# A gated linear attention with an expert layer on one core: the fourth head pair packed into unused partitions, and a new written order

## The chip, the cores and the metric

The kernel runs on one core of a Trainium2 chip. Its time is the device time in microseconds, median over runs. The engines are PE (TensorE, with PEld for its weight loads), DVE (VectorE), ACT (ScalarE), POOL (GpSimd) and SP (SyncE, which here issues every transfer).

## What is computed

```python
state = zeros((4, 8, 48, 48))                        # batch, heads, 48 x 48
for t in range(768):
    state = alpha[:, :, t, :, None] * state + einsum('bhd,bhe->bhde', k[:, :, t], v[:, :, t])
    y[:, :, t] = einsum('bhd,bhde->bhe', q[:, :, t], state)
x = y.transpose(0, 2, 1, 3).reshape(3072, 384)       # float32
h = x @ w_in                                         # w_in 384 x 2048, float64
g = h * erf(maximum(h, 0) + log1p(exp(-abs(h))))
out = (g @ w_out).astype(float32)                    # w_out 2048 x 384, float64
```

## The kernel before

**Attention.** The recurrence is cut into 24 chunks: 2 pairs of batches by 12 stretches of 64 tokens. A chunk holds 2 batches and the 8 heads as 4 head pairs. Rows of k, q and alpha lie on partitions, two halves of 64, of which 48 carry a head's rows and 16 are unused; the 512 columns are 4 pairs x 2 batches x 64 tokens. `la`, `lq`, `lv` load tiles `A`, `kq`, `raw_v`. `a1` is a scan along the tokens (DVE, L239). `a2` has three ACT steps (Relu with a sum, Ln, Exp with a sum: L245, L203) and three DVE products, of which the last, L257, makes the keys in `kq`; `a3` makes the queries (L262). `a4` multiplies keys by queries pair by pair into `pS` (PE, L277), and the chunk before's keys by its values into `pu` (L286); then DVE brings the state `T` up to date (L302, L304) and masks `pS` into `sT` (L307), PE transposes the keys (`pn`, L315) and ACT copies them out (`kn`, L320). `a5` forms the chunk's outputs `py` (PE, L343) from `T`, the queries, `sT` and `raw_v`, splits them in two parts `x_hi` (ACT, L369) and `x_lo` (DVE, L373), and two chunks make a block of 256 tokens.

**Expert layer.** Each of 12 blocks has 4 groups `g` of 512 hidden columns in two halves. A step `H` is 18 PE products `ph` (L407: three for each of 3 row tiles of w_in and 2 column tiles) and a copy `hs` (ACT, L415); `U`, `L1`, `L2`, `G`, `Z` are tanh, two logarithms and an exponential, and products on ACT and DVE; `O` splits the result in `gh` (L460 on DVE or L462 on ACT) and `gl` (DVE, L465) and makes 12 PE products `acc` (L476): per tile of 128 tokens `gh` by `wo_hi`, `gh` by `wo_lo`, `gl` by `wo_hi`. Eight steps `O` make the output of a block, and `out` copies and stores it. Where the text says the **seventh O**, it means the seventh step `O` in PE's queue, counted from the start of the program.

**Weights.** w_in comes in 12 pieces of 128x512, w_out in 16 of 128x384, as 64-bit words. `weight()` loads a piece (`wst`), ACT turns the high words into float32 (L502), DVE shifts the low words (L505) and joins them in two steps (L509, L513), ACT rounds to the high part (`wi_hi`, `wo_hi`, L518), DVE subtracts for the low part (`wi_lo`, `wo_lo`, L520).

**Order.** A table `SCHED` names the steps one after another; each name runs its step up to the next `yield`. This sets every engine's queue. `lq`, `wst`, `wbuf`, `hs`, `s`, `w`, `t` share 19 buffers of one pool, `A` has 3 buffers, `raw_v` 2, and PSUM holds 2 tiles for `ph` and 4 for attention.

Of the kernel before, what the change touches and what calls it, by code (L numbers as in the profile page):

```python
# [25 lines left out]

SCHED = """
la_0 a1_0 a2_0 la_1 a2_0 a2_0 la_2 a1_1 a1_2 lq_0 a3_0 a2_0 wi_9 wi_9 wi_9 a2_0 wi_9 wi_5 wi_5 wi_5 a2_1 a2_1 a2_0
a4_0 wi_11 wi_11 wi_9 wi_11 wi_9 wi_5 wi_11 wi_8 wi_8 a2_1 wi_8 wi_0 wi_0 lv_0 wi_0 wi_5 a4_0 a5_0 a4_0 wi_0 a2_1 wi_4
wi_4 wi_4 wi_9 a5_0 a5_0 a5_0 wi_10 wi_10 wi_10 a2_1 wi_8 a4_0 lq_1 a3_1 a2_1 wi_5 wi_11 wi_1 a2_2 a2_2 wi_1 wi_1 wi_4  # L30
wo_0 a2_2 a2_2 wi_11 wi_11 lq_2 a2_2 wi_4 wi_4 wi_2 wi_2 wi_2 wo_2 wo_5 wo_5 wi_1 a4_1 wo_13 a4_1 a4_1 a4_1 wi_0 wi_0
lv_1 a5_1 wi_4 wi_2 wi_1 wi_1 a5_1 a5_1 wo_5 wi_8 wi_3 a4_1 wi_3 wo_5 wi_6 wi_2 wi_3 wi_2 wi_1 a5_1 a5_1 lq_3 wi_0
wi_2 a5_0 H_0_0_0 wi_6 wi_3 wi_6 a2_2 a3_2 a4_2 wo_1 wo_1 wo_1 wi_5 wo_4 H_0_0_1 H_0_0_1 wi_8 la_3 wo_11 wo_11 wo_11
wi_3 wi_3 a1_3 a2_3 a2_3 a2_3 a4_2 a4_2 wi_10 wo_5 wo_5 wo_13 wo_2 wi_10 H_0_0_0 H_0_0_0 wi_3 wi_10 a2_3 wo_11 a2_3
a4_2 a4_2 wo_1 wi_7 wi_7 wi_7 H_0_0_1 wi_10 wo_7 wo_7 wo_7 wo_4 wo_4 lv_2 a5_2 wi_8 wo_4 wo_0 wo_0 wo_13 a3_3 a5_2
a5_2 a5_2 H_0_1_1 U_0_0 lv_3 wi_6 H_0_1_0 H_0_1_0 H_0_1_0 a2_3 H_0_1_1 H_0_1_1 U_0_1 L1_0_1 la_4 a1_4 a2_4 a2_4 wo_10
H_0_3_1 H_0_3_1 wo_2 H_0_3_1 wo_10 wo_10 H_0_3_0 a4_3 a5_2 wo_2 wi_6 wo_2 wi_7 wo_4 wi_7 wi_7 H_0_3_0 H_0_3_0 wo_0
a4_3 a4_3 a2_4 lq_4 a3_4 a4_3 a4_3 wi_7 wi_6 a2_4 wi_6 a5_3 a2_4 wo_13 wo_0 a2_4 L1_0_0 a5_3 H_0_2_0 a5_3 L1_0_1 a5_3
L1_0_1 L1_0_0 wo_0 L1_0_0 la_5 a1_5 a2_5 a2_5 a2_5 wo_7 H_0_2_0 H_0_2_0 wo_0 a5_3 L2_0_1 wo_5 wo_4 lv_4 a4_4 a4_4 a4_4
a4_4 a4_4 a2_5 L2_0_1 H_1_2_1 H_1_2_1 wo_4 wo_3 G_0_1 lv_5 Z_0_1 L2_0_0 H_0_2_1 H_0_2_1 wo_1 H_0_2_1 U_0_2 a5_4 a5_4  # L40
a5_4 wo_3 wo_3 H_1_2_1 L2_0_0 lq_5 wo_3 H_1_0_1 H_1_0_1 G_0_0 Z_0_0 a5_4 a2_5 H_1_1_1 wo_2 H_1_0_1 H_1_1_1 Z_0_0 a3_5
O_0_0_0 H_1_1_1 a2_5 wo_11 U_0_3 L1_0_2 H_1_0_0 H_1_0_0 H_1_0_0 wo_1 L1_0_2 H_1_1_0 L1_0_3 wo_10 wo_11 O_0_0_0 Z_0_1
la_6 wo_2 H_1_1_0 O_0_0_1 H_1_1_0 a4_5 H_1_3_1 H_1_3_1 a1_6 H_1_3_0 H_1_3_0 a2_6 wo_7 L1_0_2 O_0_0_0 wo_7 wo_3 a2_6
a2_6 wo_13 wo_13 wo_11 wo_6 a4_5 a4_5 wo_10 a4_5 wo_6 a4_5 H_1_3_1 a5_5 a5_5 wo_1 O_0_0_0 O_0_0_1 O_0_0_1 wo_3 L2_0_2
wo_3 O_0_0_1 a2_6 a5_5 a5_5 a5_5 wo_9 a5_4 H_2_1_0 H_2_1_0 L1_0_3 wo_8 wo_10 wo_10 L1_0_3 wo_6 H_1_3_0 L2_0_3 H_1_2_0
G_0_3 wo_6 H_2_1_0 wo_7 H_1_2_0 la_7 H_2_3_1 H_2_3_1 wo_6 wo_13 L2_0_2 O_0_1_0 wo_6 wo_6 O_0_1_1 a2_6 O_0_1_0 O_0_1_1
lq_6 lv_6 a1_7 O_0_1_0 O_0_1_0 O_0_1_1 O_0_1_1 G_0_2 U_1_0 L2_0_3 L1_1_0 wo_9 wo_9 a2_6 H_1_2_0 H_2_2_0 H_2_2_0 wo_14
wo_14 wo_14 a3_6 a4_6 H_2_3_1 L1_1_0 wo_8 wo_8 wo_9 L1_1_0 Z_0_2 wo_8 Z_0_2 H_2_1_1 H_2_1_1 a2_7 a2_7 a2_7 wo_14 U_1_3
H_2_1_1 a4_6 a4_6 wo_8 wo_8 Z_0_3 O_0_2_0 O_0_2_1 a4_6 a4_6 a5_6 lq_7 a3_7 wo_8 H_2_2_0 wo_12 wo_9 la_8 wo_9 O_0_2_0
a5_6 a5_6 U_1_2 a2_7 L2_1_0 G_1_0 wo_9 H_2_0_1 H_2_0_1 H_2_0_1 O_0_2_1 H_2_2_1 H_2_2_1 H_2_2_1 wo_12 O_0_2_0 L2_1_0  # L50
a5_6 wo_12 O_0_2_0 wo_12 U_1_1 a2_7 a2_7 Z_0_3 L1_1_1 O_0_3_0 a5_6 wo_14 O_0_2_1 O_0_2_1 wo_12 H_2_3_0 L1_1_2 wo_15
wo_15 lv_7 H_2_3_0 H_2_3_0 O_0_3_1 a1_8 a2_8 wo_15 L1_1_1 a4_7 a4_7 a4_7 O_0_3_0 O_0_3_1 a4_7 wo_12 H_2_0_0 H_2_0_0
H_2_0_0 L1_1_3 wo_14 L1_1_3 a5_7 a5_7 wo_12 wo_15 wo_15 wo_14 Z_1_0 wo_15 wo_15 O_0_3_0 O_0_3_0 O_0_3_1 a5_7 a5_7 a5_7
O_0_3_1 Z_1_0 lq_8 a3_8 L1_1_3 lv_8 H_3_2_1 H_3_2_1 a2_8 a2_8 a2_8 H_3_0_0 H_3_0_0 a2_8 O_1_0_0 a4_7 L1_1_1 la_9 a2_8
L1_1_2 L2_1_3 out_0_0 O_1_0_1 out_0_0 L2_1_1 out_0_1 out_0_1 L2_1_3 a4_8 H_3_2_1 H_3_1_0 H_3_1_0 O_1_0_0 L1_1_2
O_1_0_1 O_1_0_0 O_1_0_0 O_1_0_1 O_1_0_1 G_1_1 U_2_0 L2_1_1 Z_1_1 H_3_0_0 H_3_1_0 U_2_3 G_1_3 Z_1_1 O_1_1_0 O_1_1_1
L2_1_2 G_1_2 a1_9 U_2_1 L1_2_1 H_3_2_0 H_3_2_0 L1_2_0 H_3_2_0 O_1_1_0 O_1_1_1 L2_1_2 H_3_3_1 O_1_1_0 lv_9 L1_2_0 a2_9
# [655 lines left out]
```

## Time and profile before

| what | us |
|---|---|
| median of 3 runs (lowest, highest) | 537.72 (537.54, 538.38) |
| the profiled execution | 537.11 |
| its span in the trace | 535.4 |
| busy in the span: PE, PEld | 498.9, 482.1 |
| busy in the span: DVE, ACT | 485.2, 492.8 |

The span runs from the first to the last instruction that the trace shows; the profiled execution took 1.7 us more than its span, and the median is 0.6 us above that execution. PE's products overlap, so PE's busy time counts a product from its start to its modelled end; what a product costs in a full queue is the distance from one start to the next.

### The profile page before, as it was taken

The page shows a single profiled execution, that of the slowest core. Times are in us where ns is not written, and L with a number is a line of the kernel's source. Part 1 is how long each engine was busy: PE and PEld are TensorE (multiplying, and loading weights), DVE is VectorE, ACT ScalarE, POOL GpSimd, SP SyncE. Part 2 cuts the span into 40 slices and gives each one's busy share as a digit, 9 for nine tenths or more (in the row PEclk, how much of TensorE's full clock was granted, in tenths as well). Part 3 has the DMA queues.
Part 4 walks back from the last instruction along what each step waited for, and adds up shares of the span by engine and source line. Part 5 has one row for each costly group of instructions (what it writes and reads, how often), then busy time and mean ns, then how long its engine had stood idle before and what let it go on. Part 6 is the DMA issues. An engine that isn't in the chain of part 4 may idle for free.

```text
span 535.4 us, 16828 instructions
## 1 busy us (share of the span) xinstructions
PE 498.9 (93%) x7386; PEld 482.1 (90%) x7386; DVE 485.2 (91%) x684; ACT 492.8 (92%) x727; POOL 2.3 (0%) x14
## 2 busy tenths in 40 slices
...
GB/s 293 408 281 152 104 118 67 149 98 151 67 109 117 24 112 104 37 42 86 131 6 124 57 136 31 63 121 49 86 2 20 107 37 31 2 1 29 31 2 36
DMA packets 17937, 48.45 MB, mean 90 GB/s; under 512 B 1984, under 2 KB 5056, under 8 KB 17856
## 3 DMA queue, kind: packets, MB, share of 16 engines
...
q14 instruction: 21, 0.17, 0.1%
...
## 4 chain that ended last, share of the span: by engine, by line
PE 78%; ACT 7%; DVE 7%; DMA 3%; issue 2%; SPq 1%
PE acc L476 35%; PE ph L407 32%; PE py L343 5%; PE pS L277 3%; PE pu L286 2%; DMA wst<-in_moe_w_in_dram 2%; ACT s L203 2%; PE pn L315 1%; DMA raw_v<-in_v_dram 1%; ACT w L203 1%; ACT hs L415 1%; DVE wbuf L509 1%; DVE wi_lo L520 1%; DVE gl L465 1%; ACT L202 1%
## 5 line engine op out<-in xcount | busy, mean ns | idle before, releaser
L407 PE MATMUL ph<-x_hi,wi_hi 128*128 128x256 f32 x576 | 164.9, 286 | 2.1 <-ACT hs L415 1.1
L407 PE MATMUL ph<-x_lo,wi_hi 128*128 128x256 f32 x576 | 161.3, 280 | 3.2 <-DVE x_lo L373 3.2
L407 PE MATMUL ph<-x_hi,wi_lo 128*128 128x256 f32 x576 | 161.2, 280 | 0.3 <-DVE wi_lo L520 0.3
L476 PE MATMUL acc<-wo_hi,gh 128*128 128x384 f32 x384 | 131.3, 342 | 0.8 <-ACT gh L462 0.4
L476 PE MATMUL acc<-wo_hi,gl 128*128 128x384 f32 x384 | 129.7, 338 | 0.8 <-DVE gl L465 0.6
L476 PE MATMUL acc<-wo_lo,gh 128*128 128x384 f32 x384 | 129.1, 336 | 0.0
L407 PEld LDWEIGHTS ph<-x_hi,wi_hi 128*128 128x128 f32 x576 | 108.5, 188 | 5.0 <-ACT hs L415 2.0
L407 PEld LDWEIGHTS ph<-x_lo,wi_hi 128*128 128x128 f32 x576 | 108.6, 189 | 3.5 <-DVE x_lo L373 3.5
L407 PEld LDWEIGHTS ph<-x_hi,wi_lo 128*128 128x128 f32 x576 | 109.7, 190 | 0.5 <-DVE wi_lo L520 0.5
L203 ACT ACTIVATE s<-s 128x1024 f32<-128x1024 f32 x96 | 100.9, 1057 | 0.9 <-DVE t L436 0.4
L465 DVE TENSOR_TENSOR gl<-hs,gh 128x512 fp32r<-128x512 f32 x96 | 64.5, 687 | 18.6 <-ACT gh L462 16.3
L476 PEld LDWEIGHTS acc<-wo_hi,gh 128*128 128x128 f32 x384 | 72.2, 188 | 2.2 <-ACT gh L462 0.5
L476 PEld LDWEIGHTS acc<-wo_hi,gl 128*128 128x128 f32 x384 | 72.2, 188 | 2.2 <-DVE gl L465 2.2
L476 PEld LDWEIGHTS acc<-wo_lo,gh 128*128 128x128 f32 x384 | 72.2, 188 | 0.0
L436 DVE TENSOR_TENSOR t<-s,w 128x1024 f32<-128x1024 f32 x48 | 58.2, 1220 | 5.0 <-ACT w L203 4.8
L202 ACT ACT_TABLE_LOAD x48 | 61.6, 1283 | 0.8
L447 DVE TENSOR_TENSOR s<-s,w 128x1024 f32<-128x1024 f32 x48 | 58.5, 1221 | 2.7 <-ACT s L203 1.6
L449 DVE SCALAR_TENSOR_TENSOR hs<-s,hs 128x1024 f32<-128x1024 f32 x48 | 58.6, 1220 | 0.6
L438 DVE SCALAR_TENSOR_TENSOR w<-t,w 128x1024 f32<-128x1024 f32 x48 | 58.5, 1220 | 0.5
L415 ACT ACTIVATE hs<-ph 128x512 f32<-128x512 f32 x96 | 55.4, 589 | 1.8 <-PE ph L407 1.6
L462 ACT ACTIVATE gh<-hs 128x512 fp32r<-128x512 f32 x72 | 44.6, 625 | 9.5 <-DVE hs L449 7.9
L277 PE MATMUL pS<-kq 48*64 48x64 f32 x768 | 38.3, 235 | 15.3 <-DVE kq L257 15.1
...
## 6 DMA issues: line engine op xcount, KB each, us to landing
...
A<-in_alpha_dram SPq DMA_DIRECT2D x24, 260.0 KB, 3.2
...
out_dram<-o SPq DMA_DIRECT2D x24, 192.0 KB, 2.0
```

Of the source, the lines that this page charges most:

```text
L202: nc.scalar.preload_act_table_set(table)
L203: nc.scalar.activation(*args, **kw)
L277: nc.tensor.matmul(out=ps[half * HD : (half + 1) * HD, pair * NI + i, :], lhsT=K[rows, pair, i, :], rhs=Q[rows, pair, i, :], start=True, s ...
L407: nc.tensor.matmul(out=o, lhsT=wt[:, kt, fs], rhs=xt[:, kt, :], start=n == 0, stop=n == 3 * KT - 1)
L415: nc.scalar.activation(self.hs[g][:, sl], ph, AF.Copy)
L436: nc.vector.tensor_tensor(out=t, in0=s, in1=w, op=ALU.mult)
L438: nc.vector.scalar_tensor_tensor(out=w, in0=t, scalar=2.0, in1=w, op0=ALU.add, op1=ALU.mult)
L447: nc.vector.tensor_tensor(out=s, in0=s, in1=w, op=ALU.mult)
L449: nc.vector.scalar_tensor_tensor(out=h, in0=s, scalar=RT2 / 2, in1=h, op0=ALU.subtract, op1=ALU.mult)
L462: nc.scalar.activation(ghf, gg, AF.Copy)
L465: nc.vector.tensor_tensor(out=gl.rearrange("p a t -> p (a t)"), in0=gg, in1=ghf.bitcast(F32), op=ALU.subtract)
L476: nc.tensor.matmul(out=self.acc[tt][:, :DM], lhsT=gt[:, u, ts], rhs=wt[:, f, :], start=f == 0 and n == 0, stop=f == NF - 1 and n == 2,)
```

## The change

The 48 rows of each half's fourth pair are put, 16 rows by 16 rows, under the rows 48 to 63 of the first three pairs when the inputs are laid out. So `A` has 390 columns instead of 520, and `a1`, `a2`, `a3` work on 384 columns instead of 512. A new step `mv` issues six transfers within SBUF that bring the fourth pair's keys and queries back to their own place in `kq` (and each chunk's last column of `A`, which `a3` now copies behind the keys). `a4`'s first part ends ahead of the fourth pair. Three transposes take the place of four, `kn` is one tile, zeroed once, that two copies fill, and some `py` products have 16 columns of weights instead of 32. A helper `copy()` runs a copy on ACT or, where the table has `v:` ahead of a step, on DVE. In `weight()`, `v:` ahead of the third part puts the low words' conversion on ACT (L550) in place of the shift on DVE. The table is written anew (1940 steps, 138 of them with `v:`; 1846 before).

```diff
+    def copy(out, in_, scale=1.0):
+        if not on_vector[0]:
+            nc.scalar.activation(out, in_, AF.Copy, scale=scale)
+        elif scale == 1.0:
+            nc.vector.tensor_copy(out=out, in_=in_)
+        else:
+            nc.vector.tensor_scalar(out=out, in0=in_, scalar1=scale, scalar2=None, op0=ALU.mult)
...
+    kn = at.tile([P, H * D + HD - D], F32, name="kn", tag="kn")
+    nc.gpsimd.memset(kn, 0.0)
...
-    PIECES = (((0, 0),), ((1, 16),), ((0, 32), (1, -16)))
+    PIECES = (((0, 0, 32),), ((1, 16, 32),), ((1, -16, 32), (0, 32, 16)))
...
-            r = at.tile([P, NP * NI, TC], F32, name="r", tag="r")
+            r = at.tile([P, NX, NI, TC], F32, name="r", tag="r")
...
         def a3(self):
-            qq = self.kq[:, 1].rearrange("p a i t -> p (a i) t")
-            nc.vector.tensor_tensor(out=qq, in0=qq, in1=self.A[:, :, 1:], op=ALU.mult)
+            qq = self.kq[:, 1, :NX, : NI * TC].rearrange("p a (i t) -> p a i t", i=NI)
+            nc.vector.tensor_tensor(out=qq, in0=qq, in1=self.A[:, :, :, 1:], op=ALU.mult)
+            yield
+            copy(self.kq[:, 0, :NX, NI * TC :], self.A[:, :, :, TC])
+            yield
+
+        def mv(self):
+            rows = self.kq.rearrange("(b r) w a t -> b r w a t", b=2)
+            for j in range(NX):
+                n = D // NX
+                for b in range(2):
+                    nc.sync.dma_start(out=rows[b, j * n : (j + 1) * n, :, NX, :], in_=rows[b, D:, :, j, :])
             yield
...
             for pair in range(NP):
+                if pair == NX:
+                    yield
                 for i in range(NI):
...
-                for pair in range(NP):
+                for pair in range(NX):
                     nc.tensor.transpose(
...
-                self.kn = at.tile([P, NP, 2, HD], F32, name="kn", tag="kn")
-                nc.scalar.activation(self.kn.rearrange("p a b d -> p (a b d)"), pn, AF.Copy)
+                by_pair = pn[:, : NX * P].rearrange("p (a b d) -> p a b d", a=NX, b=2)
+                knv = kn[:, : H * D].rearrange("p (a b d) -> p a b d", a=NP, b=2)
+                copy(knv[:, :NX], by_pair[:, :, :, :D])
+                yield
+                copy(knv[:, NX].rearrange("p b (a d) -> p a b d", a=NX), by_pair[:, :, :, D:])
                 yield
...
-            if half == 0 and g % 2 == 0:
-                nc.vector.tensor_copy(out=ghf, in_=gg)
-            else:
-                nc.scalar.activation(ghf, gg, AF.Copy)
+            copy(ghf, gg)
...
-            nc.scalar.activation(y, high, AF.Copy, scale=2.0**-112)
...
+        copy(y, high, sign * 2.0**-112)
...
+        if on_vector[0]:
+            nc.scalar.activation(z, low.bitcast(U32), AF.Copy, scale=0.937 * 2.0**-29)
+        else:
+            nc.vector.tensor_scalar(out=z, in0=low, scalar1=29, scalar2=None, op0=ALU.logical_shift_right)
...
+            on_vector[0] = step[:2] == "v:"
+            step = step.removeprefix("v:")
...
-la_0 a1_0 a2_0 la_1 a2_0 a2_0 la_2 a1_1 a1_2 lq_0 a3_0 a2_0 wi_9 wi_9 wi_9 a2_0 wi_9 wi_5 wi_5 wi_5 a2_1 a2_1 a2_0
+la_0 la_1 a1_0 a1_1 la_2 a1_2 a2_0 a2_0 lq_0 a3_0 a3_0 wi_1 a2_0 a2_0 a2_0 a2_0 wi_1 v:wi_1 a2_1 a2_1 a2_1 wi_1 lq_1
...
+H_6_3_0 a2_16 a2_15 mv_15 a4_15 a4_15 Z_4_3 L1_5_2 Z_5_0 Z_5_0 v:O_4_3_0 v:O_4_3_1 O_4_3_0 a2_16 a2_16 L1_5_1 L1_5_1
```

ACT's queue at the start of the program, before (L502 is the high words' conversion, L518 the rounding of a weight, L245 and L203 are `a2`):

```order
L203 ACTIVATE r<-A 128x512
L203 ACTIVATE r,flags<-r 128x512
L502 ACTIVATE wbuf<-wst 128x512 x2
L245 ACTIVATE r,flags<-A 128x512
L203 ACTIVATE r<-A 128x512
L502 ACTIVATE wbuf<-wst 128x512
L518 ACTIVATE wi_hi<-wbuf 128x512
L502 ACTIVATE wbuf<-wst 128x512
L203 ACTIVATE r,flags<-r 128x512
```

And the same place after the change (L219 stands for every `copy()` on ACT, L550 is the low words' conversion, L266 and L213 are `a2`):

```order
L213 ACTIVATE r<-A 128x384
L219 ACTIVATE kq<-A 128x3x2
L213 ACTIVATE r,flags<-r 128x384
L219 ACTIVATE wbuf<-wst 128x512
L550 ACTIVATE wbuf<-wst 128x512
L266 ACTIVATE r,flags<-A 128x384
L213 ACTIVATE r<-A 128x384
L213 ACTIVATE r,flags<-r 128x384
L219 ACTIVATE wi_hi<-wbuf 128x512
L219 ACTIVATE wbuf<-wst 128x512
L550 ACTIVATE wbuf<-wst 128x512
```

A piece of weight has two conversions behind each other on ACT where it had one, and chunk 0 has the small copy `kq<-A`.

SP's queue, the transfers from the ninth on, before, with the semaphores that each waits for (DMAHW0 to DMAHW7 count finished transfers, DVE and PE finished instructions):

```order
L497 DMA wst_173<-in_moe_w_in_dram 128x1024 [waits DMAHW0_49]
L234 DMA raw_v_177<-in_v_dram 128x896 [waits DMAHW1_49]
L497 DMA wst_227<-in_moe_w_in_dram 128x1024 [waits DMAHW2_49]
L497 DMA wst_236<-in_moe_w_in_dram 128x1024 [waits DMAHW3_49]
L226 DMA kq_245<-in_qk_dram 128x1024 [waits DMAHW4_49]
```

And after the change (`kq<-kq` are the transfers of `mv_0`):

```order
L250 DMA kq_158<-in_qk_dram 128x1040 [waits DMAHW0_49]
L244 DMA A_167<-in_alpha_dram 128x390 [waits DMAHW1_49,DVE_49]
L255 DMA raw_v_186<-in_v_dram 128x896 [waits DMAHW2_49]
L293 DMA kq_121<-kq_121 16x2x130 [waits DMAHW3_49,DVE_49]
L293 DMA kq_121<-kq_121 16x2x130 [waits DMAHW4_49]
L293 DMA kq_121<-kq_121 16x2x130 [waits DMAHW5_49]
L293 DMA kq_121<-kq_121 16x2x130 [waits DMAHW6_49]
L293 DMA kq_121<-kq_121 16x2x130 [waits DMAHW7_49]
L293 DMA kq_121<-kq_121 16x2x130 [waits DMAHW0_49]
L540 DMA wst_212<-in_moe_w_in_dram 128x1024 [waits DMAHW1_49]
```

The six transfers of `mv_0`, the first of which waits for DVE, stand ahead of the fourth weight's load.

PE's queue at chunk 15 after the change, with what each waits for (`pu` are the products of chunk 14's keys and values):

```order
L447 MATMUL ph<-x_hi,wi_lo 128x256
L311 MATMUL pS<-kq 64x64 [waits DMAHW4_49,DVE_49]
L311 MATMUL pS<-kq 64x64 x3
L320 MATMUL pu<-raw_v,kn 64x48 x4
L311 MATMUL pS<-kq 64x64 x4
L320 MATMUL pu<-raw_v,kn 64x48 x4
L311 MATMUL pS<-kq 64x64 x4
L320 MATMUL pu<-raw_v,kn 64x48 x4
L311 MATMUL pS<-kq 64x64 [waits DMAHW6_49,DMAHW4_49,DMAHW2_49]
L311 MATMUL pS<-kq 64x64 [waits DMAHW7_49,DMAHW5_49,DMAHW3_49]
L311 MATMUL pS<-kq 64x64 x2
L320 MATMUL pu<-raw_v,kn 64x48 x4
L513 MATMUL acc<-wo_hi,gh 128x384 [waits DVE_49]
```

Before, no `pS` product but the first of a chunk waited for anything of that chunk; now the fourth pair's wait for the six transfers, and between them and chunk 15's first `pS` product PE has only eleven `pS` and twelve `pu` products to do.

## Rows read from the trace of the kernel before

**Rows 1.** The profile's busy time by stretch, cut at the first `gl` product of the seventh step `O`; columns: the stretch, its length, then busy us (and instructions) of PE, PEld, DVE, ACT and POOL, the granted clock, the busy share of the DMA engines, GB/s.
```profile
0.00:10.00 10.00, 0.00 (x0) 0.00 (x0) 5.44 (x7) 5.15 (x8) 2.35 (x14) 1.00 0.83 261
10.00:129.20 119.20, 100.56 (x1978) 93.94 (x1979) 118.08 (x215) 104.76 (x183) 0.00 (x0) 1.00 0.49 172
129.20:510.00 380.80, 380.45 (x5312) 371.83 (x5312) 347.33 (x448) 370.74 (x523) 0.00 (x0) 1.00 0.20 65
```

**Rows 2.** The waits of the first 100 us, engine and line that waited, releaser: total us, times, longest.
```profile
PE pS L277 <- DVE kq L257: 15.1, 2, 12.1
...
ACT wi_hi L518 <- DVE wbuf L513: 5.0, 4, 2.4
...
ACT wbuf L502 <- DVE wi_lo L520: 3.3, 1, 3.3
```

**Rows 3.** Timeline of PE: the second `ph` product of the run, the first `pS` product of chunk 3, the first `gl` product of the seventh step `O`, four transposes (`x4`) with their neighbours, the first `pS` product of chunk 18; columns here and in the next groups: start us, duration us, engine, line, operation, tiles, shapes.
```profile
34.88 0.58 PE L407 MATMUL ph<-x_lo,wi_hi 128*128 128x256 f32 x1 [3.20 <-DVE x_lo L373]
...
54.74 0.39 PE L277 MATMUL pS<-kq 48*64 48x64 f32 x6
...
129.21 0.34 PE L476 MATMUL acc<-wo_hi,gl 128*128 128x384 f32 x1
...
302.65 0.28 PE L407 MATMUL ph<-x_lo,wi_hi 128*128 128x256 f32 x1
302.76 0.28 PE L407 MATMUL ph<-x_hi,wi_lo 128*128 128x256 f32 x1
302.88 0.60 PE L315 MATMUL pn<-ident,kq 128*128 128x128 f32 x4
303.24 0.42 PE L476 MATMUL acc<-wo_hi,gh 128*128 128x384 f32 x1
...
336.99 0.33 PE L277 MATMUL pS<-kq 48*64 48x64 f32 x3
```

**Rows 4.** Timeline of DVE: places with two elementwise steps behind each other, and the last key product of chunks 3 and 18.
```profile
41.02 0.68 DVE L307 TENSOR_TENSOR sT<-pS,maskn 128x512 f32<-128x512 f32 x1
41.62 0.68 DVE L509 SCALAR_TENSOR_TENSOR wbuf<-wbuf 128x512 int32<-128x512 int32 x1
...
44.49 0.55 DVE L509 SCALAR_TENSOR_TENSOR wbuf<-wbuf 128x384 int32<-128x384 int32 x1
44.96 0.68 DVE L254 SCALAR_TENSOR_TENSOR rw<-rw,r 128x512 f32<-128x512 f32 x1
...
46.03 0.43 DVE L505 TENSOR_SCALAR wbuf<-wst 128x512 int32<-128x512 int32 x1
46.38 0.68 DVE L520 TENSOR_TENSOR wi_lo<-wbuf,wi_hi 128x512 fp32r<-128x512 f32 x1
...
50.61 0.67 DVE L257 TENSOR_TENSOR kq<-kq,rw 128x512 f32<-128x512 f32 x1
...
331.93 0.69 DVE L257 TENSOR_TENSOR kq<-kq,rw 128x512 f32<-128x512 f32 x1
```

**Rows 5.** Timeline of ACT at the start.
```profile
4.92 0.63 ACT L245 ACTIVATE r<-A 128x512 f32<-128x512 f32 x1 [2.83 <-DVE A L239]
...
9.49 0.68 ACT L502 ACTIVATE wbuf<-wst 128x512 f32<-128x512 f32 x1 [1.15 <-DMA wst<-in_moe_w_in_dram]
...
12.62 0.67 ACT L502 ACTIVATE wbuf<-wst 128x512 f32<-128x512 f32 x1
13.18 0.62 ACT L518 ACTIVATE wi_hi<-wbuf 128x512 fp32r<-128x512 f32 x1
13.70 0.66 ACT L502 ACTIVATE wbuf<-wst 128x512 f32<-128x512 f32 x1
```

**Rows 6.** Groups of instructions over the whole run, different shapes apart: line, engine, operation, tiles, shapes, count | busy us, mean ns of one | idle us before them and its releasers.
```profile
L202 ACT ACT_TABLE_LOAD x48 | 61.6, 1283 | 0.8
...
L239 DVE TENSOR_TENSOR_SCAN A<-A,lower 128x520 f32<-128x520 f32 x24 | 29.5, 1234 | 3.7 <-DMA A<-in_alpha_dram 3.6
L343 PEld LDWEIGHTS py<-kq,T 48*32 48x32 f32 x1408 | 24.9, 107 | 3.8 <-issue 1.3 <-PE pn L315 0.4 <-PE acc L476 0.2
...
L343 PEld LDWEIGHTS py<-sT,raw_v 64*32 64x32 f32 x1536 | 23.8, 108 | 5.0 <-DVE sT L307 2.9 <-DVE rw L252 1.3 <-DMA raw_v<-in_v_dram 0.6
...
L460 DVE CAST gh<-hs 128x512 fp32r<-128x512 f32 x24 | 10.2, 425 | 1.7 <-PE acc L476 0.5
...
L502 ACT ACTIVATE wbuf<-wst 128x384 f32<-128x384 f32 x16 | 8.5, 550 | 3.6 <-DVE wi_lo L520 3.3 <-DMA wst<-in_moe_w_out_dram 0.4
L518 ACT ACTIVATE wo_hi<-wbuf 128x384 fp32r<-128x384 f32 x16 | 8.3, 516 | 0.7 <-DVE wbuf L513 0.7
...
L505 DVE TENSOR_SCALAR wbuf<-wst 128x384 int32<-128x384 int32 x16 | 5.3, 347 | 0.0
L505 DVE TENSOR_SCALAR wbuf<-wst 128x512 int32<-128x512 int32 x12 | 5.1, 423 | 0.2 <-DMA wst<-in_moe_w_in_dram 0.2
```

**Rows 7.** DMA: two rows of the page's list of DMA issues (count, KB each, median us from issue to landing), and SP's first issues.
```profile
A<-in_alpha_dram SPq DMA_DIRECT2D x24, 260.0 KB, 3.2
...
out_dram<-o SPq DMA_DIRECT2D x24, 192.0 KB, 2.0
...
0.82 1.34 SPq L221 DMA_DIRECT2D A<-in_alpha_dram  x3
...
13.53 0.33 SPq L226 DMA_DIRECT2D kq<-in_qk_dram  x1
```

More of the change, by code (lines that the diff above doesn't have):

```diff
@@ L14 @@
 I32 = mybir.dt.int32
+U32 = mybir.dt.uint32
 AMIN = 1e-18
@@ L185, in gla_moe @@
     nc.gpsimd.memset(flags, 0.0)
-    lower = const.tile([P, NP * NI, 1 + TC], F32, name="lower")
+    lower = const.tile([P, NX, NI, 1 + TC], F32, name="lower")
     nc.gpsimd.memset(lower, AMIN)
-    nc.gpsimd.memset(lower[:, :, 0], 1.0)
+    nc.gpsimd.memset(lower[:, :, :, 0], 1.0)
     wi_hi = const.tile([P, KT, FF], F32R, name="wi_hi")
@@ L237, in a1 @@
         def a1(self):
-            a, floor = (z.rearrange("p s t -> p (s t)") for z in (self.A, lower))
+            a, floor = (z.rearrange("p a i t -> p (a i t)") for z in (self.A, lower))
             nc.vector.tensor_tensor_scan(out=a, data0=a, data1=floor, initial=1.0, op0=ALU.mult, op1=ALU.max)
```

372 lines of the change are left out of this document (199 added, 173 removed).

## The prediction

> **What bounds the kernel now.** I read the busy time by stretch first. From 129.2 us to 510 us PE has 380.45 busy of 380.80 us, while DVE has 347.33 and ACT 370.74 [rows 1]: there the queue of PE's products is the time, and nothing that ACT or DVE saves shows. Ahead of 129.2 us it is otherwise: DVE is busy 5.44 + 118.08 = 123.5 of 129.2 us, ACT 5.15 + 104.76 = 109.9, and PE only 100.6, so PE is idle 28.6 us [rows 1]. The waits name whom they wait for: PE 15.1 us for the key product on DVE, ACT 5.0 us for a weight's joining on DVE and 3.3 us for a buffer that DVE's subtraction sets free [rows 2]. The start belongs to DVE, the rest to PE. So I split the time at one place that both versions have, the first `gl` product of the seventh O, at 129.21 us before [rows 3], and ask two things: how much earlier PE comes there, and how much work it has left.
>
> **Prices.** What a step costs in a full queue is the distance to the next start. On DVE 512 columns cost 0.60 (41.02 to 41.62), 384 columns 0.47 (44.49 to 44.96), the shift of 512 columns 0.35 (46.03 to 46.38) [rows 4] and of 384 columns 0.35 - 0.08 = 0.27, by the difference of 423 and 347 ns [rows 6]. On ACT a conversion of 512 columns costs 0.56 (12.62 to 13.18), a rounding 0.52 (13.18 to 13.70) [rows 5]; with 384 columns they take 550 and 516 ns busy [rows 6], 0.12 and 0.11 less than the 0.67 and 0.62 at 512 [rows 5], so 0.44 and 0.41. On PE an H product costs 0.23 / 2 = 0.115 and a transpose 0.36 / 4 = 0.09 [rows 3].
>
> **DVE ahead of the seventh O.** The queues of both versions, counted up to that product: 24 shifts leave (12 x 0.35 + 12 x 0.27 = -7.4), 32 products shrink to 384 columns (32 x 0.13 = -4.2), nine scans from 520 to 390 columns (a quarter of 1234 ns [rows 6], -2.8), and seven copies come from ACT (+1.9, a copy at 425 ns busy [rows 6]). Together -12.5: 123.5 becomes 111.0 us.
>
> **ACT ahead of the seventh O.** 24 more conversions (12 x 0.56 + 12 x 0.44 = +12.0), `a2` with 27 steps at 0.41 for 25 at 0.52 (-1.9), five roundings gone to DVE (-2.3), seven small copies of columns (+0.5), `kn` in two copies of 288 and 96 columns for one of 512 (0), and expert steps that now stand behind the place (three of 1024 columns and a `gh` copy, less an `hs` and an `x_hi` copy, -2.7). Together +5.6: 109.9 becomes 115.5 us. ACT takes DVE's place as the engine with the most to do there.
>
> **When PE comes there.** ACT cannot begin its first weight ahead of 9.49 us, by when it has idled 9.49 - 4.64 = 4.9 us [rows 1, 5]; with no further wait it would be done at 120.4. With all the 19.3 us of idle time that it has now [rows 1] it would be 134.8. Most of that idle time was waiting for a full DVE [rows 2], which now has 18 us to spare, so I take a third of the 14.4 us between: 125.0, a gain of 4.2 us. PE's own queue allows it: 36 H products are moved ahead of the place (+4.1) and eight transposes are gone (-0.7), which its 28.6 us of idle time can hold; its H products began in earnest at 34.88 us, behind a wait for DVE's `x_lo` [rows 3].
>
> **What PE has left.** 36 H products fewer (-4.1) and 14 transposes fewer (22 in all, x 0.09 = -1.3): -5.4. The table loads of ACT rise from 49 to 65 in the queues, all behind this place, 16 x 1283 ns [rows 6] = 20.5 us more; conversions, `gh` and `o` copies that go to DVE and the narrower `a2` make up for it, and by my count ACT ends with some 362 and DVE with some 364 us for PE's 387 there. They stay under PE, so I cost these at nothing; if one copy in four of those moved to DVE took the 0.68 of a read from PSUM [rows 4] instead of 425 ns, DVE would lose under 6 us of its 22 us of cover.
>
> **The unknown prices.** The low words' conversion reads integers, which no row of before does: as cheap as a rounding (0.52) or as dear as the other conversion (0.56), nearest to the latter, since tile and stride are the same; twice that would put 12 us on ACT ahead of the seventh O. The copy of six columns lies between nothing and the 0.41 of 384 columns, 2.9 us for seven; it is nearest to the lower end, and 0.07 is taken. The 16-column `py` products halve a quarter of weight loads that are busy 24.9 + 23.8 us [rows 6]: a gain from 0 to 6 us. Their moving side has not changed and PE's own busy time is the fuller, so I take 0 and keep 6 for the range.
>
> **The six transfers per chunk.** SP issues one in 0.33 [rows 7] to 0.45 us (1.34 / 3 [rows 7]), and a transfer lands in 2.0 (`out`) to 3.2 us (`A`) [rows 7]. The sixth has landed 5 x 0.33 + 2.0 = 3.7 to 6 x 0.45 + 3.2 = 5.9 us after the last key product; being small, they are nearest to `out`, and with a half for the wake-up I take 4.2. What covers this is PE's work between. In before, PE's first `pS` product began 3.5 us (51.28 to 54.74, chunk 3) to 4.4 us (332.62 to 336.99, chunk 18) after that product's end [rows 3, 4], on average 2.8 us over these sixteen chunks; the products written between the two steps come to 3.1 at the prices above. So the written order is a fair measure. The new one has between the last key product and the fourth pair, for chunks 3 to 18: 10.8, 10.5, 6.6, 5.2, 15.9, 7.3, 4.2, 1.1, 10.4, 9.2, 6.3, 11.8, 1.1, 7.3, 9.7 and 10.8 us; later ones have over 20, and chunks 0 to 2 lie where PE is idle anyway. Two, chunks 10 and 15, are short (the order of PE at chunk 15 shows it). In before, where nearly nothing stood between, PE came some 1.2 us later than written, so 2.3 against 4.2: 1.9 us twice, +3.8 us. Free at the best; at 5.9 us and without the 1.2, 0.7 + 1.7 + 4.8 + 4.8 = 12 us.
>
> The Trainium skill ("DMA: Bandwidth & Descriptors", Rules for kernel authors) speaks against this step: many small transfers should be made one large one, since under 64 KB they are mostly overhead, and each has about 2.0 us of fixed cost (Anatomy of one DMA). The 192 KB store that lands in 2.0 us [rows 7] agrees with a floor near that. If the floors of six overlap, the sum is mine; if they came one after another, 12 us by an estimate from that page, it would be the slower rival below, larger.
>
> **The sum.** 535.4 - 4.2 - 5.4 + 3.8 = 529.6 us of span. The profiled execution of before took 1.7 us more than its span, and its median lies 0.6 above it, so 531.9 us.
>
> **Rivals.**
> (a) Better, under 528: copies under cover and 16-column products worth some us. 529.6 - 3.8 = 525.8 of span is 528.1; with half of the 6 us, 525. For it: PE often lags behind the written order. Against it: no row prices these products.
> (b) Small gain or no change: ACT gains nothing at the start. Its queue is longer than before, four weights wait behind `mv_0` in SP's queue, and that waits for DVE; with 10 us of idle time more than the 4.9, PE is at the seventh O at 130.4, and the sum ends at 537.3. For it: every weight now passes ACT three times. Against it: DVE's queue there shrinks by a tenth.
> (c) Slower: PE waits for the fourth pair in most chunks. It is nothing up to 4.2 us, costs 12 at 5.9 and decides from about 5.5 us (9.6 us of waits use up both gains); at 8 us the chunks' shortfalls are 1.4, 2.8, 0.7, 3.8, 6.9, 1.7, 6.9 and 0.7 = 25 us, the time 553. For it: each of the six holds one of eight counters that the next transfers wait for, and other transfers stand ahead of `mv` in SP's queue. Against it: the DMA engines are only 20% busy there [rows 1].
> (d) The conversion of integers on ACT is twice as dear: +12 us at the start, 543.
>
> **How the numbers follow.** Forecast (528 to 535) 0.50, (a) 0.17, (b) 0.16, of which half within 0.2%, (c) 0.13, (d) 0.04. A difference of 0.2%, 1.1 us, is about what a measurement here can tell from none. So faster 0.75, the same 0.08, slower 0.17. The range from 524 to 540 leaves out the far end of (a) and most of (c) and (d).
>
> **What would show it.** The seventh O near 125 us; conversions of low words near 0.56 apart; `pS` waits for DMA of some 4 us in sum, in chunks 10 and 15; PE full from there to 500; DVE's idle time at the start up by some 8 us. I am wrong if ACT or DMA waits put that place at 129 or later, if `pS` waits for DMA in most chunks, or if ACT's table loads leave PE waiting for `gh` or `x_hi` in the middle.

## The result, and the profile after

The changed kernel takes 544.73 us (544.0 to 545.64, four runs) where the kernel before takes 538.05 (537.54 to 539.85): ratio 1.0119, 95% interval 1.0087 to 1.0150. The profiled execution took 545.64 us, its span is 543.9. The forecast was 531.9 us with a range from 524 to 540, so it was wrong in size and in sign.

The same cut as in [rows 3] comes first, the first `gl` product of the seventh O, and then the busy time on both sides of it, as in [rows 1].

```profile
132.75 0.34 PE L513 MATMUL acc<-wo_hi,gl 128*128 128x384 f32 x1
```

```profile
0.00:132.75 132.75, 106.08 (x2007) 100.48 (x2007) 112.92 (x206) 115.63 (x226) 2.61 (x15) 0.99 0.55 181
132.75:543.90 411.15, 400.19 (x5359) 389.22 (x5358) 377.43 (x541) 371.75 (x502) 0.00 (x0) 0.99 0.19 62
```

PE comes to the seventh O 3.5 us later than before (129.21), not 4.2 earlier, though DVE (112.9) and ACT (115.6) did the work that was foretold (111.0 and 115.5). What is left takes 411.15 us where 406.2 were needed before and 406.2 - 5.4 = 400.8 were foretold. So both parts of the sum failed: 132.75 - 125.0 = 7.8 us ahead of the cut, 411.15 - 400.8 - 3.8 = 6.6 us behind it beyond the 3.8 set aside for the copies.

The waits of PE over the whole span (total us, times, longest) show a releaser that the kernel before does not have, the copies within `kq`; four rows of the list (`issue` means that the profile names nothing that PE waited for):

```profile
PE pS L311 <- DMA kq<-kq: 13.1, 7, 6.1
PE pS L311 <- DVE kq L278: 9.9, 1, 9.9
PE py L383 <- issue: 2.8, 2, 1.9
PE py L383 <- DMA raw_v<-in_v_dram: 1.9, 1, 1.9
```

13.1 us are spent on the fourth pair's copies, 9.9 of them in the first 60 us. Then SP's own view of these copies: how long each issue takes (ns, least, median, most), and how long from an issue to the landing; first for all 144, then for the 18 of chunks 0 to 2.

```profile
L293 SPq DMA_DIRECT2D kq<-kq x144: 585/591/1672, 9.9 to 447.0; - x144
...
DMA to landing us min/median/max: 1.8/1.9/7.3
...
L293 SPq DMA_DIRECT2D kq<-kq x18: 585/591/1040, 9.9 to 33.0; - x18
...
DMA to landing us min/median/max: 2.7/5.8/7.3
```

An issue of 16 partitions by two pieces takes 0.59 us, not the 0.33 to 0.45 of a whole tile [rows 7]. The median landing, 1.9 us, is what was foretold, but not at the start: there the DMA engines are busy (a share of 0.55 ahead of the cut, 0.19 behind it, in the rows above) and it takes 2.7 to 7.3 us. In chunks 0, 1 and 2 it was 7.7, 11.6 and 14.0 us from the last key product to PE's product; chunk 2's keys were ready at 22.40, its first copy was issued at 27.65, behind other transfers in SP's queue, and its last one landed at 36.46.

Two later chunks where PE waited, with DVE's last key product, the copy of the end columns (ACT or DVE), SP's issues and the product of the fourth pair at which PE's wait ended:

```profile
69.61 0.55 DVE L278 TENSOR_TENSOR kq<-kq,rw 128x384 f32<-128x384 f32 x1
...
70.67 0.24 ACT L219 ACTIVATE kq<-A 128x6 f32<-128x6 f32 x1
...
70.93 4.35 SPq L293 DMA_DIRECT2D kq<-kq  x6
...
78.20 0.27 PE L311 MATMUL pS<-kq 48*64 48x64 f32 x2 [1.46 <-DMA kq<-kq]
```

```profile
205.27 0.16 DVE L221 COPY kq<-A 128x6 f32<-128x6 f32 x1
...
210.31 0.55 DVE L278 TENSOR_TENSOR kq<-kq,rw 128x384 f32<-128x384 f32 x1
...
205.46 9.48 SPq L293 DMA_DIRECT2D kq<-kq  x12
...
218.33 0.41 PE L311 MATMUL pS<-kq 48*64 48x64 f32 x6 [1.24 <-DMA kq<-kq]
```

In chunk 5 the copies begin only at 70.93, since they also carry the end columns, which ACT copies at 70.67, behind another step; from the end of the last key product (70.16) to PE's product it is 8.0 us. In chunk 12 it is 7.5 us (210.86 to 218.33). Chunk 11's six copies had waited for their end columns until 205.43 and stand in the same row, but they were issued by 210.32 and chunk 12's first one began at 210.88, at once behind its key product: they did not hold it up. What both chunks share is the landing of the last copy, chunk 5's issued at 74.68 and chunk 12's at 214.35:

```profile
DMA to landing us min/median/max: 3.4/3.4/3.4
...
DMA to landing us min/median/max: 3.8/3.8/3.8
```

With 1.9 us these two would have landed at 76.6 and 216.3; PE came to the products that needed them at 76.74 and 217.09. So, by these numbers, PE would not have waited in either chunk with the usual landing, nor, by an estimate, with issues of 0.33 us, which bring the last one 1.8 to 2.1 us forward (5 x 0.33 in place of 3.47 and 3.75). In both, the trace has the copy's last two packets of 520 bytes start at 76.94 and 217.00, where a packet of 16 KB on the DMA queue that brings instructions (begun at 76.00 and 215.67) ended at 76.94 and 217.01.

Behind each of these two waits PE's granted clock falls (columns as in [rows 1], the clock third from the right), and the products show it. First the two stretches, then products at the fall and, for comparison, at full clock:

```profile
80.00:82.50 2.50, 2.50 (x13) 2.50 (x13) 2.50 (x4) 1.31 (x2) 0.00 (x0) 0.50 0.45 163
...
220.00:222.50 2.50, 2.50 (x13) 2.50 (x13) 2.40 (x3) 2.50 (x5) 0.00 (x0) 0.50 0.36 138
```

```profile
219.01 0.28 PE L447 MATMUL ph<-x_hi,wi_lo 128*128 128x256 f32 x1
219.13 0.28 PE L447 MATMUL ph<-x_hi,wi_hi 128*128 128x256 f32 x1
...
220.22 0.41 PE L447 MATMUL ph<-x_hi,wi_hi 128*128 128x256 f32 x1
220.44 0.41 PE L447 MATMUL ph<-x_lo,wi_hi 128*128 128x256 f32 x1
...
278.79 0.29 PE L447 MATMUL ph<-x_hi,wi_lo 128*128 128x256 f32 x1
278.92 0.28 PE L447 MATMUL ph<-x_hi,wi_hi 128*128 128x256 f32 x1
279.03 0.28 PE L447 MATMUL ph<-x_lo,wi_hi 128*128 128x256 f32 x1
279.15 0.28 PE L447 MATMUL ph<-x_hi,wi_lo 128*128 128x256 f32 x1
```

At 220 us the H products stand 0.22 apart, at the lower of the clock's two levels (granted share 0.50, 1.2 GHz). The granted share over the stretches from 77.5 to 85 and from 217.5 to 225 us is 0.88, 0.50, 0.94 and 0.87, 0.50, 0.95: 2.5 x (0.12 + 0.50 + 0.06) = 1.7 us each. Not every such wait has a drop behind it. In this trace PE also stood still for 1.95 us ahead of 193.32, and the granted share stayed at 1.00; in the run `after_x64` below, chunk 5 had a longer wait and no drop behind it:

```profile
193.32 0.41 PE L383 MATMUL py<-sT,raw_v 64*16 64x64 f32 x24 [1.95 <-issue]
...
80.36 0.27 PE L313 MATMUL pS<-kq 48*64 48x64 f32 x2 [1.62 <-DMA kq<-kq]
...
80.00:82.50 2.50, 2.13 (x29) 2.11 (x30) 1.59 (x4) 2.14 (x5) 0.00 (x0) 1.00 0.21 27
```

The products from 278.79 on show something that no step of the prediction looked for: at full clock the H products stand 0.12 apart (278.79 to 279.15, three in 0.36), where before it was 0.115 [rows 3]. The mean over the run, taken from all distances under 0.3 us, is 0.119 before and 0.124 after, the drops of the clock among them; the median, which the drops do not move, is 0.117 and 0.120; the weight loads, by their group, take 193 ns where they took 188 to 190:

```profile
L447 PEld LDWEIGHTS ph<-x_hi,wi_hi 128*128 128x128 f32 x576 | 111.4, 193 | 2.0
```

1728 products by 0.003 to 0.004 us are 5 to 7 us at the most.

### The profile page after: what moved, and what is told of

It is laid out like the page before. It is cut to its first block, busy times and chain, and to the rows that moved or that the text cites. A ratio compares the mean times of both kernels' runs of the same rounds, so it can differ in the third digit from the quotient of the medians.

```text
span 543.9 us, 17103 instructions
## 1 busy us (share of the span) xinstructions
PE 506.3 (93%) x7364; PEld 489.7 (90%) x7364; DVE 490.3 (90%) x746; ACT 487.4 (90%) x727; POOL 2.6 (0%) x15
## 4 chain that ended last, share of the span: by engine, by line
PE 69%; ACT 11%; DMA 8%; DVE 5%; SPq 3%; issue 2%; ACTq 0%; DVEq 0%
PE ph L447 30%; PE acc L513 29%; PE py L383 4%; PE pS L311 3%; DMA kq<-kq 2%; ACT w L213 2%; ACT s L213 2%; SPq L293 2%; DMA wst<-in_moe_w_out_dram 2%; PE pu L320 2%; ACT hs L219 1%; DMA raw_v<-in_v_dram 1%; DMA wst<-in_moe_w_in_dram 1%; ACT L212 1%; PE pn L350 1%
## 5 line engine op out<-in xcount | busy, mean ns | idle before, releaser
L447 PE MATMUL ph<-x_hi,wi_hi 128*128 128x256 f32 x576 | 168.2, 292 | 0.0
L447 PE MATMUL ph<-x_hi,wi_lo 128*128 128x256 f32 x576 | 164.2, 285 | 0.0
L447 PE MATMUL ph<-x_lo,wi_hi 128*128 128x256 f32 x576 | 164.1, 285 | 0.0
L513 PE MATMUL acc<-wo_hi,gh 128*128 128x384 f32 x384 | 130.4, 340 | 0.0
L447 PEld LDWEIGHTS ph<-x_hi,wi_hi 128*128 128x128 f32 x576 | 111.4, 193 | 2.0
L447 PEld LDWEIGHTS ph<-x_lo,wi_hi 128*128 128x128 f32 x576 | 111.4, 193 | 0.0
L447 PEld LDWEIGHTS ph<-x_hi,wi_lo 128*128 128x128 f32 x576 | 111.3, 193 | 0.0
L213 ACT ACTIVATE s<-s 128x1024 f32<-128x1024 f32 x96 | 101.2, 1057 | 3.8 <-DVE t L476 3.3
L502 DVE TENSOR_TENSOR gl<-hs,gh 128x512 fp32r<-128x512 f32 x96 | 65.0, 687 | 9.0 <-ACT gh L219 6.0
L219 ACT ACTIVATE hs<-ph 128x512 f32<-128x512 f32 x82 | 47.9, 591 | 17.9 <-PE ph L447 17.8
L311 PE MATMUL pS<-kq 48*64 48x64 f32 x768 | 41.7, 235 | 23.8 <-DMA kq<-kq 13.1
L311 PEld LDWEIGHTS pS<-kq 48*64 48x64 f32 x768 | 34.6, 143 | 29.3 <-DVE kq L278 9.9
## 6 DMA issues: line engine op xcount, KB each, us to landing
kq<-kq SPq DMA_DIRECT2D x144, 16.2 KB, 1.9
```

The source lines that it names most:

```text
L213: nc.scalar.activation(*args, **kw)
L219: nc.scalar.activation(out, in_, AF.Copy, scale=scale)
L311: nc.tensor.matmul(out=ps[half * HD : (half + 1) * HD, pair * NI + i, :], lhsT=K[rows, pair, i, :], rhs=Q[rows, pair, i, :], start=True, s ...
L447: nc.tensor.matmul(out=o, lhsT=wt[:, kt, fs], rhs=xt[:, kt, :], start=n == 0, stop=n == 3 * KT - 1)
L502: nc.vector.tensor_tensor(out=gl.rearrange("p a t -> p (a t)"), in0=gg, in1=ghf.bitcast(F32), op=ALU.subtract)
L513: nc.tensor.matmul(out=self.acc[tt][:, :DM], lhsT=gt[:, u, ts], rhs=wt[:, f, :], start=f == 0 and n == 0, stop=f == NF - 1 and n == 2,)
```

## The experiments

Theory B: the copies are the price, by SP's time to issue them, what stands behind them in SP's queue, and PE's waits. Theory A: the H products are slower because `x_hi` and `x_lo` lie elsewhere. The tiles' places are those in the built program: tiles ahead of them became narrower, and so `x_hi` starts at byte 123776 of each partition, 128 modulo 256, where it started at 127296, 64 modulo 256. `lower`, `A`, `r` and `rw` gave up whole multiples of 256 bytes (3072 together); it is the new `kn`, 400 columns where it had 512 (448 bytes), that changes the place modulo 256; the weights start at 128 modulo 256 in both, `gh` and `gl` at 64 in both.

**No copies** (the fourth pair stays as loaded).

```diff
         def mv(self):
-            rows = self.kq.rearrange("(b r) w a t -> b r w a t", b=2)
-            for j in range(NX):
-                n = D // NX
-                for b in range(2):
-                    nc.sync.dma_start(out=rows[b, j * n : (j + 1) * n, :, NX, :], in_=rows[b, D:, :, j, :])
             yield
```

> The changed kernel without the six transfers per chunk; the fourth pair's keys and queries stay as loaded, which leaves part of the computation out. Theory B (the transfers, issued by SP at 0.63 us each and not at 0.33 to 0.45, cost PE 13.1 us of named waits, of which 3.2 us behind the first 60 us, two drops of the granted clock behind such waits for 1.7 us each, and a longer start): 544.7 less 3.2 + 3.4 and less 3 to 6 us at the start, 532 to 538 us. Rival (the start is held by ACT and the copies hide behind it): only the 6.6 us behind the start or less, 538 us or more.

529.49 us, ratio 0.9835 (0.980 to 0.987). The seventh O comes at 123.90 and the rest takes 528.3 - 123.9 = 404.4 us:

```profile
123.90 0.34 PE L508 MATMUL acc<-wo_hi,gl 128*128 128x384 f32 x1
```

Of the 15.6 us of span that the copies cost, 132.75 - 123.90 = 8.9 lie ahead of the cut and 6.7 behind it. The copies are the price, as theory B says, and it is larger than the range given (532 to 538 us).

**Copies that nobody waits for.** They are issued at the same places and write a spare tile (the fourth pair stays as loaded).

```diff
-                    nc.sync.dma_start(out=rows[b, j * n : (j + 1) * n, :, NX, :], in_=rows[b, D:, :, j, :])
+                    nc.sync.dma_start(out=other[b, j * n : (j + 1) * n, :, : NI * TC + NI], in_=rows[b, D:, :, j, :])
```

> The changed kernel whose six transfers per chunk are issued at the same places and read the same rows, but write a spare tile that nobody reads, so that no product waits for them (the fourth pair stays as loaded, which leaves part of the computation out). Theory B1 (PE's waits for the landing are the price, with the drops of the clock behind them): close to the run without transfers, 529.5 to 532 us. Theory B2 (the transfers hold SP's queue, and weights and values behind them come late): close to the changed kernel, 539 to 545 us. The seventh O tells the start apart: 123.9 us without transfers, 132.75 with them.

536.3 us, ratio 0.9968 (0.9946 to 0.9991), between the two: neither half is all. The seventh O, two of PE's waits in the first 60 us, and the issue of the second `raw_v` on SP, without copies and then with copies that nobody waits for:

```profile
129.64 0.34 PE L515 MATMUL acc<-wo_hi,gl 128*128 128x384 f32 x1
```

```profile
PE py L385 <- DVE sT L344: 4.8, 1, 4.8
PE py L385 <- DMA raw_v<-in_v_dram: 3.9, 1, 3.9
```

```profile
15.97 0.33 SPq L255 DMA_DIRECT2D raw_v<-in_v_dram  x1
...
24.94 0.33 SPq L256 DMA_DIRECT2D raw_v<-in_v_dram  x1
```

With nobody waiting for the copies, the cut still comes 129.64 - 123.90 = 5.7 us late: that is SP's queue, where weights and `raw_v` stand behind the copies (the second `raw_v` is issued 9.0 us later, and PE waits 3.9 us for it, a row that the run without copies does not have). Behind the cut it costs only 0.8 us (534.8 - 129.64 = 405.2 against 404.4). What the products' waiting adds is the rest: 132.75 - 129.64 = 3.1 us ahead and 411.15 - 405.2 = 6.0 us behind. These are single executions, and one kernel run twice below differs by 2.6 us at the seventh O, so the 3.1 us are hardly clear of that.

Of the 6.0 us behind the cut, the trace names 1.7 us of waits for copies and 1.7 us of clock. Another 0.7 us, in chunk 14, has no releaser named, but the last copy landed at 261.16 and PE went on at 261.25. The 1.95 us ahead of 193.32 have no releaser named either, and nothing shows that the copies cause them: the runs with two queues below, where no product waits for a copy at that time, have such a wait too (1.3 to 2.4 us). Each of these ended 2.4 to 2.8 us after a 16 KB packet began on the queue that brings instructions (190.66 in this trace). That they are waits for instructions was not tested.

**Copies on two queues.** POOL, which is idle, issues the three of the second half. First with `x_hi` and `x_lo` back at 64 modulo 256, then without and with that on one chip, then all six on POOL (with it).

```diff
+    at.tile([P, 48], F32, name="pad_x", tag="pad_x")
+    big.tile([P, 16], F32, name="pad_b", tag="pad_b", bufs=1)
...
-                    nc.sync.dma_start(out=rows[b, j * n : (j + 1) * n, :, NX, :], in_=rows[b, D:, :, j, :])
+                    (nc.sync, nc.gpsimd)[b].dma_start(out=rows[b, j * n : (j + 1) * n, :, NX, :], in_=rows[b, D:, :, j, :])
```

> The changed kernel with x_hi and x_lo at 64 modulo 256 (as in after_x64) and the three transfers of the second half issued by POOL, which is idle, in place of SP. If SP's time to issue (six times 0.59 to 0.63 us behind each other, and every load behind them) is the price, the last transfer lands 1.9 us earlier and loads are not held: 532 to 538 us against 544.0 for after_x64, at or under the kernel before. If the landing or POOL's own issue is slower than SP's, 542 us or more.

> The changed kernel with nothing but the second half's three transfers issued by POOL in place of SP; x_hi and x_lo stay at 128 modulo 256. If the transfers' issue on one queue was the price, 532.1 (copies_split) plus the 2 to 4 us of the slower H products: 533 to 537 us, against 544.7 as changed. If copies_split owes its gain to the place of x, 542 us or more.

> copies_split once more, beside split_only on the same chip, for a closer interval: 530 to 534 us, ratio 0.985 to 0.993 to the kernel before, and 2 to 4 us under split_only.

> x at 64 modulo 256, and all six transfers of a chunk issued by POOL, 0.51 us each, so that no load stands behind them on SP. If the loads behind them on SP are what is left of the price, 528 to 532 us; if PE's wait for the last landing is (six behind each other again, 3.1 + 1.9 us), 534 to 540 us.

| kernel | us | ratio to before (95%) | seventh O |
|---|---|---|---|
| copies_split | 532.08 | 0.9898 (0.9869 to 0.9926) | 122.57 |
| split_only | 535.49 | 0.9943 (0.9923 to 0.9963) | 125.25 |
| split_x64 | 531.5 | 0.9858 (0.9824 to 0.9893) | 125.21 |
| all_on_pool | 536.75 | 0.9965 (0.9943 to 0.9987) | 127.99 |

The issues of `copies_split`, and PE's waits behind 130 us of it and of `all_on_pool`:

```profile
L295 SPq DMA_DIRECT2D kq<-kq x72: 585/592/1662, 10.6 to 428.3; - x72
L295 POOL DMA_DIRECT2D kq<-kq x72: 504/507/639, 11.3 to 428.3; - x72
```

```profile
PE ph L449 <- issue: 1.3, 1, 1.3
PE acc L515 <- DVE gl L504: 1.3, 3, 0.5
PE ph L449 <- ACT hs L219: 0.6, 2, 0.4
```

```profile
PE pS L313 <- DMA kq<-kq: 2.7, 3, 1.4
PE acc L515 <- DVE gl L504: 0.7, 2, 0.5
PE ph L449 <- ACT hs L219: 0.4, 2, 0.3
```

With two queues no product behind 130 us waits for a copy (`split_only` has no such row either), and 544.73 become 535.49 us with nothing else changed. With all six on POOL SP's queue is free, but six issues stand behind each other again and the waits return: 5 us more than split at the same place of x, as expected of the last landing. In the two profiled executions, 3.1 us apart, 2.8 of it lie ahead of the seventh O. `copies_split` and `split_x64` are one kernel, run twice, 2.6 us apart at the seventh O and 0.6 us at the end; it is faster than both kernels that this document compares.

**The place of x_hi and x_lo.** Unused bytes ahead of them move them, and as many behind as make up 256 keep `gh` and `gl` at 64. `r`, `rw` and `sT` (and `kn` in the kernel before) lie between and move along; the H products read none of these. The diff is that of `before_x128` (64 bytes ahead, 192 behind); the others differ from it in the two sizes alone.

```diff
+    at.tile([P, 16], F32, name="pad_x", tag="pad_x")
+    big.tile([P, 48], F32, name="pad_b", tag="pad_b", bufs=1)
```

> The changed kernel with two unused pieces of SBUF (192 bytes per partition ahead of the tiles x_hi and x_lo, 64 behind them), so that these start at 64 modulo 256 bytes per partition, as in the kernel before, in place of 128; the order and all else stay. Theory A (the H products run at 0.122 us in place of 0.118 all through the run because of where their operands lie): mean weight load of L447 back from 193 to 188-190 ns, pitch 0.118, 1728 x 0.004 = 6.9 us less, 537 to 539 us. Rival (they are slower because other engines or transfers disturb them, whatever the place): 193 ns and 544 to 546 us as before the edit.

> The kernel before with 64 unused bytes ahead of x_hi and x_lo and 192 behind, so that they start at 128 modulo 256 as in the changed kernel. Theory A: its H products slow down to a pitch of 0.122, weight loads 193 ns, and the time rises by about 6.9 us to 544 to 546 us. Rival: 188 to 190 ns and 537 to 539 us, no change.

> The changed kernel with x_hi and x_lo at 0 modulo 256 (128 unused bytes ahead, 128 behind). Theory A leaves open which places are good: if only the distance to the weights (wi_hi and wi_lo start at 128 modulo 256) matters, 0.118 and 537 to 539 us; if 64 alone is good, 0.122 and 544 to 546 us. Rival: 544 to 546 us.

> The kernel before with x_hi and x_lo at 192 modulo 256 bytes (before: 64; at 128 it was 542.2 us with a pitch of the H products of 0.122, at 64 0.118). If odd multiples of 64 are the good places, 0.118 and 537 to 539 us; if it is the distance in steps, 0.120 or more and 540 us or more; below 537 us would be a better place than both kernels have.

> The changed kernel without transfers (part of the computation is left out) and with x_hi and x_lo at 64 modulo 256: both causes taken away. If they add up, 529.5 less 4 to 6 us, 523.5 to 526 us, and the H products at 0.118; if the slower H products were hidden, 528 to 530 us.

| kernel | x modulo 256 | distance of H products: mean | median | us | ratio to before (95%) |
|---|---|---|---|---|---|
| before | 64 | 0.1187 | 0.117 | 538.05 | |
| before_x128 | 128 | 0.1225 | 0.120 | 542.23 | 1.0067 (1.0036 to 1.0097) |
| before_x192 | 192 | 0.1211 | 0.118 | 540.11 | 1.0038 (1.0024 to 1.0052) |
| after | 128 | 0.1239 | 0.120 | 544.73 | 1.0119 (1.0087 to 1.0150) |
| after_x64 | 64 | 0.1200 | 0.117 | 544.0 | 1.011 (1.0041 to 1.018) |
| after_x0 | 0 | 0.1221 | 0.119 | 543.49 | 1.011 (1.0068 to 1.0151) |
| after_no_copies | 128 | 0.1233 | 0.120 | 529.49 | 0.9835 (0.980 to 0.987) |
| no_copies_x64 | 64 | 0.1203 | 0.117 | 527.28 | 0.9797 (0.9779 to 0.9816) |

The weight loads of `before_x128` and of `after_x64`, by their groups:

```profile
L409 PEld LDWEIGHTS ph<-x_hi,wi_hi 128*128 128x128 f32 x576 | 110.5, 192 | 3.9 <-ACT hs L417 1.0 <-ACT x_hi L371 0.9 <-ACT wi_hi L520 0.4
```

```profile
L449 PEld LDWEIGHTS ph<-x_lo,wi_hi 128*128 128x128 f32 x576 | 109.1, 189 | 0.0
```

Moving x makes the kernel before slower by 0.67% and its H products slower by 0.003 us at the median, and moving it back in the changed kernel brings the products back to 0.117. The places 0 and 192 lie between. The runs of the other sections agree: 0.117 at 64 (`copies_split`, `split_x64`, `all_on_pool`, `split_shift_dve`), 0.120 at 128 (`copies_unread`, `split_only`). So the place matters, by what it does to these products: 2 to 4 us of the time (542.23 against 538.57, the median of before on that chip; 529.49 against 527.28; 535.49 against 531.5). In the changed kernel itself the gain did not show: with the copies on one queue, 544.0 and 544.73 us can't be told apart. Its runs spread from 539.93 to 546.74, and its profile has 2.4 us of waits for `hs` between 60 and 130 us that the changed kernel's lacks. The forecast of 6.9 us was too large (`no_copies_x64` gained 2.2 us where 4 to 6 were expected), and why 64 is the best of the four places stays open.

With both causes taken away the span is 525.5 us, the seventh O at 122.88 and the rest 402.6 us.

**The low words back on DVE.** `copies_split` with the shift in place of ACT's conversion.

```diff
-        if on_vector[0]:
+        if False:
```

> copies_split with the low words' shift back on DVE at the same places of the order (26 more instructions on DVE, 26 conversions fewer on ACT). If the start belongs to whichever of the two has the most to do, DVE's 112.9 us of work ahead of the seventh O become 120 and with 5.7 us of idle time the seventh O comes at 125 to 127 us in place of 122.6, the time 534 to 537 us. If the start is set by transfers and by the order alone, 122 to 123 and 530 to 534 us.

535.23 us, ratio 0.9927 (0.990 to 0.9954), against 531.5 to 532.1 with the conversions on ACT, and the seventh O falls back further than expected:

```profile
131.08 0.34 PE L515 MATMUL acc<-wo_hi,gl 128*128 128x384 f32 x1
```

So giving ACT this work brings the seventh O forward by 5.9 to 8.5 us (131.08 against 125.21 and 122.57), of which 3 to 4 are left at the end.

## Why the prediction was wrong

**Right: where the time is set, and the two gains.** The start depended on DVE, and the work of both engines there came out within 2 us of the count. With both causes taken away the span of 525.5 us is the sum without its copy term (535.4 - 4.2 - 5.4 = 525.8), though the parts differ: the seventh O at 122.88 in place of 125.0, the rest 402.6 in place of 400.8. Two errors of about 2 us cancel, so that the sums agree to 0.3 us is luck.

**Right: most of the unknown prices.** The conversion of integers costs what the other conversion costs, so rival (d) is out; the 16-column products load their weights in 93 and 92 ns in place of 108 and 107 [rows 6], with no gain on PE (the `py` steps behind the cut take 22.2 us without copies, 22.3 before, by the distances from start to start):

```profile
L550 ACT ACTIVATE wbuf<-wst 128x512 int32<-128x512 uint32 x12 | 7.9, 661 | 0.0
L219 ACT ACTIVATE wbuf<-wst 128x512 f32<-128x512 f32 x12 | 8.0, 665 | 1.6 <-DMA wst<-in_moe_w_in_dram 1.4
L219 ACT ACTIVATE kq<-A 128x6 f32<-128x6 f32 x18 | 3.7, 207 | 0.6 <-DMA kq<-in_qk_dram 0.6
L383 PEld LDWEIGHTS py<-sT,raw_v 64*16 64x16 f32 x384 | 6.7, 93 | 2.2 <-issue 2.1
L383 PEld LDWEIGHTS py<-kq,T 48*16 48x16 f32 x352 | 5.2, 92 | 0.0
```

Behind the cut ACT and DVE had 371.8 and 377.4 us of work, 10 and 13 more than counted, and stayed under PE as said. Two slips of the prediction carry nothing: a third of 14.4 us puts the seventh O at 125.2 and not 125.0, and PE's 387 us of work behind it come out of no row (it was busy 398.3 us there before; 5.4 less is 392.9).

**Wrong: the six transfers per chunk**, the term of 3.8 us that measures 15.2 (544.73 - 529.49). Five things in that step failed.
- The price of an issue was taken from rows of whole tiles. It is 0.59 us, and 4.35 us for six in chunk 5, so the last of six is issued 3.5 to 3.8 us behind the first (chunks 12 and 5), not 1.7.
- The landing was taken at 2.0 us, at most 3.2. The median is 1.9, but the last copy took 3.4 and 3.8 us in chunks 5 and 12, and the copies of chunks 0 to 2 took 2.7 to 7.3.
- What the copies wait for was taken to be the last key product. They also carry the end columns, and a copy on ACT or DVE that stands behind other work held them (chunk 5 by 0.8 us; chunk 11 by 6.7 us, at no cost to PE). From the key product to PE's use it was 8.0 and 7.5 us in chunks 5 and 12, and 7.7 to 14.0 us in chunks 0 to 2, where 4.2 was assumed and 5.9 was the bound.
- What covers them was read from the written order and named chunks 10 and 15. No wait stands there; the longest ones behind the start are in chunks 5 and 12, with 6.6 and 9.2 us written (chunk 12 had 6.2 in the trace).
- The cost at the start was put at nothing because PE is idle there anyway. But SP's queue is the one that brings the weights: 5.7 us are lost at the seventh O even when nobody waits for the copies. The prediction saw the four weights behind `mv_0`, but priced them only within rival (b), which puts the seventh O at 130.4; it came at 132.75.

The time is that of rival (c), the slower one, but its mechanism is only half of what happened. The threshold of 5.5 us was passed in five chunks at least, yet PE did not wait in most chunks: the trace names a copy in seven of 24, and behind the first 60 us these waits are 3.2 us in all. The larger part is ahead of the seventh O, where (b) had the mechanism, weights held in SP's queue. Rival (c) was given 0.13 because the DMA engines were 20% busy. They were so behind 129 us; ahead of it [rows 1] has 0.83 and 0.49, and there the copies landed late. Behind it what counted was the issuing queue, one transfer behind the other, and a late last landing.

The rule of the Trainium skill ("DMA: Bandwidth & Descriptors", Rules for kernel authors) that small transfers are mostly overhead, which the prediction weighed, held: a copy of 16.2 KB landed in 1.9 us at the median, a store of 192 KB in 2.0 [rows 7]. The section of the Trainium skill from which the prediction took the 2.0 us of fixed cost (same page, Anatomy of one DMA) is on transfers that GpSimd issues; these came from SP, and the trace gives 1.9 us for them. It also shows what adds up: behind the start, landings of 1.9 us overlap, and the issues follow one another. No run here makes several copies into one.

**Wrong: nothing was said of the H products.** The change moves `x_hi` and `x_lo` in SBUF, and 576 x 3 products run some 3% slower: 2 to 4 us where a run shows it. No step of the prediction looked at places in memory.

**Not priced: the clock.** Each of two waits of 1.2 and 1.5 us was followed by a drop that cost 1.7 us more; waits as long as these, in the same trace and in other runs, had none behind them.
